# Attention with a gated residual on one Trainium2 core: output-weight sums spread over twelve blocks, and a reordered end stage

## The chip, the cores and the metric

The kernel runs on one core of one Trainium2 chip. The metric is the device time of one execution in microseconds, the median of several runs. A profile is one execution, recorded by the hardware profiler. TensorE is called PE in the profile (its weight loads PEld), VectorE is DVE, ScalarE is ACT, GpSimd is POOL and SyncE is SP; a "q" behind the name is the engine's own queue, on which DMA issues stand.

## What is computed

One sequence x of 2048 tokens with 1024 channels, all in float32. After a layer norm without gain, two branches work on the normalised xn:

```
xn  = layernorm(x)
qkv = xn @ wqkv                       # 32 heads of 32 channels
s   = softmax(q k^T / sqrt(32)) v @ wo
r   = xn @ w_r                        # one score per token
idx = the 8 tokens with the largest r
y   = (silu(xn[idx] @ w_gate) * (xn[idx] @ w_up)) @ w_down * sigmoid(r[idx])
g   = silu(xn + scatter(y at idx))
out = x + s * g
```

## The kernel before, in words

**Precision.** A float32 operand is held as two float16 parts, high and low, and a product is taken as three float16 products (high-high, high-low, low-high), each as four matmuls of 32 weight columns (`narrow`, L282). A guard at the very end checks in four conditions that the ranges allow this (denominators, their inverses, largest weights, low parts); if it fails, `_general` computes everything again.

**Attention.** The 32 heads make 8 groups g of four heads. A block (g, qb) is one group with 512 queries (qb from 0 to 3), 32 blocks in all; a block has 16 units kt, one for each 128 keys. A unit takes the scores (L282, tile `sc`), their exponential on ScalarE (L413, tile `pt`), an addition into the block's running sum of exponentials on VectorE (L420; the sum lives in the `pt` tile of unit 0, five such tiles rotate) and the product with v (L427, tile `oa`). Between these matmuls stand pieces of the next projections (`fill`).

**Denominators.** One unit after a block's end, `fold` stores the running sum into the DRAM buffer a_d (L461, on SyncE's queue) and adds its halves three times with accumulating DMAs on GpSimd's queue (L463). `fold_load` and `fold_rows` bring the 16 rows back and add them; `reciprocals` inverts on VectorE (L479), stores to r_d (L483) and loads it spread over the partitions as `rb` (L488); `normalise` multiplies (L497), `split_o` makes the two parts (L503, L505). `sums` is the other way to the denominators: four matmuls with ones into one bank (L445), a copy on ScalarE (L447), a small store and load (L452, L453). Before the change only block (7, 0) uses it. After the very last block's `rb` the whole of r_d is loaded as `rec` (L491) for the guard.

**Output projection in the end.** For query blocks 2 and 3 (the last eight tiles of 128 tokens) the projection with wo is taken as seven half-size products of sums and differences ("forms") of attention blocks (tiles `sf`, from s_d) and of wo blocks (tiles `tf`, from t_d), which VectorE puts together (L956 to L1004). The forms of wo come from t_f: for each i of 0 to 3, four planes of 512 columns of sums of wo blocks i and 4+i, made in DRAM. Before the change plane 0 holds form 3, plane 1 form 2, plane 2 form 4 and plane 3 form 1 (`T_AT`). In block (1, i) `wo_first` loads all four planes (1 MB, unit 9, SyncE, L745), and `wo_more` accumulates three planes, three planes and one plane (768, 768 and 256 KB; units 11, 13 and 15; GpSimd, L750).

**The end stage.** After the last attention unit come 79 steps on TensorE (`products`): steps 0 to 15 are form 7 (four tiles of 128 tokens, four pieces each, 12 matmuls a piece; ScalarE copies them out, L992), 16 to 27 product 4, 28 to 39 product 6, 40 to 51 product 5, 52 to 63 product 2, 64 to 72 product 3 for three tiles, 73 to 78 product 3 for the last tile in two halves of 256 columns. A tile of a product is three steps of 16 matmuls into one bank of PSUM, and three single banks rotate. After each step the functions placed there with `then(n, ...)` are issued; a function that returns (k, f) has f issued k steps later.

**Gates.** For a tile of 128 tokens `gate_load` loads x as z (L794) and, on GpSimd, clears the tile `up` (L796) and gathers the routed rows into it (L797); three `up` buffers rotate. `gate_sum` normalises z on ScalarE (L806); then one function a step: z + up on VectorE (L809), tanh on ScalarE (L813), the end of silu on VectorE (L814). Before the change the four gates of query block 3 are loaded at steps 22, 24, 26 and 28 and summed at 32, 34, 36 and 38. `written` adds the gated result to x (tile `xo`, loaded by `x_load`, L1018) on VectorE (L936) and stores it (L937).

**Order.** PE, VectorE, ScalarE, SyncE and GpSimd issue in the program order of the code up to `order.close()`. The guard stands behind that line (L1391 to L1409), and its instructions are placed by the framework: in the profile its reductions over `rec` (L1394 to L1396) stand on VectorE's queue inside product 6.

Of the kernel before, what the change touches and what calls it, by code (L numbers as in the profile page):

```python
# [9 lines left out]
F32 = mybir.dt.float32  # L10
# [4 lines left out]
ALU = mybir.AluOpType  # L15
AX = mybir.AxisListType
RED = bass_isa.ReduceOp

P = 128
S = 2048  # L20
D = 1024
# [6 lines left out]
NB = S // 512  # L28
KT = D // P
NG = H // 4  # L30
# [13 lines left out]
KSB = 8  # L44
PTB = 5
HLB = 3
# [59 lines left out]
def _fast(ctx, tc, x, wqkv, wo, w_r, w_gate, w_up, w_down, out, dram, y_d, slot_d, ok_i,  # L106
# [322 lines left out]
        if kt:  # L429
            PT.pop(u)  # L430

    DN = {}

    def unload(g, qb):

# [39 lines left out]
        return reciprocals(g, qb)  # L475

    def reciprocals(g, qb):
        dr = DN[g, qb]
        nc.vector.reciprocal(dr[:, 1], dr[:, 0])  # L479
        rows = r_d[g * NB + qb]  # L480

        def store():
            nc.sync.dma_start(rows.rearrange("j (b q) -> (j b) q", q=16), dr[:, 1])  # L483
            return 4 if (g, qb) == (L, NB - 1) else 1, spread

        def spread():
            rb = DN[g, qb] = sb.tile([P, 512], F32, name="rb", tag="rb", bufs=1)
            nc.sync.dma_start(rb, bass.AP(tensor=rows.tensor, offset=rows.offset, ap=[[512, 4], [0, 32], [1, 512]]))  # L488
            if g == NG - 1 and qb == NB - 1:
                RT["rec"] = sb.tile([P, 512], F32, name="rec", tag="hl", bufs=HLB)  # L490
                nc.sync.dma_start(RT["rec"], r_d.rearrange("b j q -> (b j) q"))  # L491

        return 1, store

    def normalise(g, qb):
        o32 = OA[g, qb]
# [54 lines left out]
    RT = {}  # L551

    def route_load(t):
        if t == 0:
# [183 lines left out]

    WO = {}

    def wo_times(k, h, n):
        return bass.AP(tensor=wo.tensor, offset=wo.offset + k * P * D + 512 * h, ap=[[D, P], [0, n], [1, 512]])
# [118 lines left out]


    SF, TF, PR, XO = {}, {}, {}, {}
    T_AT = {1: 3, 2: 1, 3: 0, 4: 2}

    def form_tiles(f, form, two, name, part=None):
        if two:
# [53 lines left out]
    def tail_items():  # L921
        items = []
        v = nc.vector
        low, high = slice(0, 512), slice(512, D)

        def row(name, tt):
            if tt == 0:
# [3 lines left out]
        def gated(y, z, scale):  # L931
            v.scalar_tensor_tensor(z, y, scale, z, op0=ALU.mult, op1=ALU.mult)

        def written(t, tt, qb):
            o = XO[qb, tt]
            v.tensor_add(o, o, GT[qb][:, tt])  # L936
            nc.sync.dma_start(out[t * P:(t + 1) * P, :], o)  # L937

        def whole(n, tt, j):


            z_a, z_b = (GT[q][:, tt] if q in GT else None for q in (2, 3))
            if j == 0:
                PR["b"] = psm.tile([P, 512], F32, name="wop", tag="m")
            bank = PR["b"]
            terms(n, tt, bank, 4 * j, 4 * j + 4)
            if j < 2:
                return
            if n == 1:
                if tt % 2 == 0:  # L950
                    PR["p1", tt // 2] = sb.tile([P, 2, 512], F32, name="p1", tag=f"w16_{tt // 2}")
                nc.scalar.activation(PR["p1", tt // 2][:, tt % 2], bank, AF.Copy)
            elif n == 4:
                if tt % 2 == 0:
                    PR["g", tt // 2] = sb.tile([P, 2, 512], F32, name="g", tag="qs", bufs=2)
                v.tensor_add(PR["g", tt // 2][:, tt % 2], PR["h"][:, tt], bank)  # L956
            elif n == 6:
                u, h, y = row("u", tt), PR["h"][:, tt], PR["g", tt // 2][:, tt % 2]
                v.tensor_tensor(u, bank, PR["p1", tt // 2][:, tt % 2], op=ALU.subtract)
                v.tensor_add(y, u, y)  # L960
                gated(y, z_a[:, low], WOD)
                v.tensor_add(h, u, h)
            elif n == 5:
                u, h = PR["u"][:, tt], PR["h"][:, tt]
                v.tensor_add(h, h, bank)
                v.tensor_add(u, u, bank)  # L966
                gated(h, z_a[:, high], -WOD)
                written(8 + tt, tt, 2)
            elif n == 2:
                y = PR["p1", tt // 2][:, tt % 2]  # L970
                v.tensor_add(y, y, bank)
                gated(y, z_b[:, low], WOD)
                if tt == 3:
                    o = XO[3, 3]
                    v.tensor_add(o[:, low], o[:, low], z_b[:, low])
                    nc.sync.dma_start(out[S - P:S, low], o[:, low])
                    u = PR["u"][:, tt]
                    gated(z_b[:, high], u, WOD)
                    v.tensor_add(o[:, high], o[:, high], u)
            elif n == 3:  # L980
                y = PR["u"][:, tt]
                v.tensor_add(y, y, bank)
                gated(y, z_b[:, high], WOD)
                written(12 + tt, tt, 3)

        def lines(i, tt):

# [24 lines left out]
        items += [lambda a=(h, j): last(*a) for h in range(2) for j in range(3)]  # L1012
        return first, items

    def x_load(qb, tt, tag):
        t = 4 * qb + tt
        XO[qb, tt] = sb.tile([P, D], F32, name="xo", tag=tag, bufs=2)
        nc.sync.dma_start(XO[qb, tt], x[t * P:(t + 1) * P, :])  # L1018


# [5 lines left out]
    def on(g, qb, kt, fn, *a):  # L1026
        side.setdefault((g, qb, kt), []).append(lambda: fn(*a))
# [111 lines left out]
    then(6, form_whole, "s", 2, False)  # L1139
    then(8, form_whole, "t", 2, False)  # L1140
    then(18, form_whole, "s", 1, True)
    then(20, form_whole, "t", 1, True)
    then(30, fold_load, L, 3)
    then(35, fold_rows, L, 3)
    then(38, form_load, L, 3)
    then(46, normalise, L, 3)
    then(47, split_o, L, 3)
    then(48, form_sum, L, 3)
    then(49, form_split, L, 3, 0, 3)
    then(44, form_tiles, SF, 4, False, "sf")  # L1150
    for i in range(4):
        then((45, 46, 47, 55)[i], form_fetch, "s", 4, i)
    for tt in range(4):
        then((30, 31, 40, 49)[tt], x_load, 2, tt, "qs" if tt == 2 else "wr")
        then((54, 55, 58, 61)[tt], x_load, 3, tt, ("wr", "qs", "qs", "wr")[tt])

# [224 lines left out]
    for n, f in enumerate(products):  # L1381
        clock[0], ready = len(units) + n, due.pop(len(units) + n, [])
        go(f)
        for h in ready + tail.pop(n, []):
            go(h)
    assert not due and not tail and not any(k[0] > L for k in side)

    order.close()


    fl = const.tile([P, 10], F32, name="fl")  # L1391
    nc.gpsimd.partition_all_reduce(am, am, channels=P, reduce_op=RED.max)
    rec = RT["rec"]
    nc.vector.tensor_reduce(fl[:, 0:1], rec, axis=AX.X, op=ALU.add)  # L1394
    nc.vector.reciprocal(rec, rec)
    nc.vector.tensor_reduce(fl[:, 1:2], rec, axis=AX.X, op=ALU.add)  # L1396
    nc.vector.tensor_reduce(fl[:, 2:3], am, axis=AX.X, op=ALU.min)
    nc.vector.tensor_scalar(fl[:, 0:1], fl[:, 0:1], REC_MAX, None, op0=ALU.is_lt)
    nc.vector.tensor_scalar(fl[:, 1:2], fl[:, 1:2], DEN_MAX, None, op0=ALU.is_lt)
    nc.vector.tensor_scalar(fl[:, 2:3], fl[:, 2:3], W_MIN, None, op0=ALU.is_ge)  # L1400
# [160 lines left out]
```

## Time and profile before

| | us |
|---|---|
| median of 3 runs | 1674.81 (1670.83 to 1676.37) |
| the profiled execution, its own time | 1679.71 |
| its span, from the first to the last instruction | 1677.9 |
| PE busy / DVE busy / ACT busy / POOL busy | 1607.2 / 1444.3 / 1195.0 / 162.7 |
| mean granted TensorE clock | 0.987 of full speed |

The profile's rows read as follows. A row of the timeline has its start, its length, the engine, the line of the code, the operation, the tiles (out<-in) and the shape; in brackets behind it stands how long the engine was idle just before and what ended that (`<-`). Times are microseconds from the start of the span. Rows of one line and shape are put together in the groups: count, total, mean in ns, idle time before. A row of the waits says who waited for what, for how long in total, how many times, and the longest. The chain is the sequence of work that ended last, each piece with its start and length. A busy PE is not PE at its peak, since the ends of matmuls are modelled.

### The profile page before, as it was taken

What the parts mean: (1) busy time and instruction counts of PE and PEld (TensorE: products, weight loads), DVE (VectorE), ACT (ScalarE), POOL (GpSimd) and SP (SyncE); (2) the same over time, 40 slices, a digit from 0 to 9 for tenths busy, and PEclk for the clock granted to TensorE, in tenths of its full rate; (3) what the DMA queues carried; (4) which work ended last, traced back from release to release, by engine and by line L of the source; (5) the groups of instructions that cost most, each with busy time, mean ns of one, the idle gap of its engine ahead of it and who ended that gap; (6) DMA issues with size and microseconds to landing.
All of it is one profiled execution on the core that took longest, in us unless ns stands there. A gap on an engine that the chain in (4) does not pass through costs nothing.

```text
span 1677.9 us, 59438 instructions
## 1 busy us (share of the span) xinstructions
PE 1607.2 (96%) x26945; PEld 830.0 (49%) x26945; DVE 1444.3 (86%) x1219; ACT 1195.0 (71%) x1339; POOL 162.7 (10%) x160
## 2 busy tenths in 40 slices
PE   9999999998899999999999999999999999999955
PEld 7644444454444455555555555555444444555522
DVE  8488999898889999999999988788899999787675
ACT  6677777777677777888888877777777778665420
POOL 3400000111000000000000000000001001212020
PEclk9999999999999999999999999999999999999979
DMA  9934565888954465667666687778888897647735
GB/s 291 201 94 134 146 165 151 206 200 192 207 133 103 118 167 150 168 171 191 165 178 172 180 249 213 206 217 203 225 238 231 235 236 241 177 138 211 270 117 184
DMA packets 272598, 313.52 MB, mean 187 GB/s; under 512 B 111702, under 2 KB 202118, under 8 KB 268370
## 3 DMA queue, kind: packets, MB, share of 16 engines
q1 hardware_dynamic: 257778, 273.68, 55.0%
q0 software_dynamic: 14560, 35.96, 13.7%
q8 instruction: 213, 3.49, 0.9%
q14 instruction: 47, 0.39, 0.1%
HBM read 224.28 MB, written 127.32 MB: 210 GB/s over the span
## 4 chain that ended last, share of the span: by engine, by line
PE 73%; DMA 14%; DVE 7%; issue 2%; SPq 2%; ACT 1%; POOL 1%; DVEq 0%; POOLq 0%; ACTq 0%
PE sc L282 22%; PE oa L427 21%; PE proj L282 15%; PE vp L282 6%; PE wop L282 5%; DMA a_d<-pt 3%; DMA a_d<-a_d 3%; DVE pt L420 3%; PE ffn L684 1%; DMA t_f<-in_A_wo_dram 1%; DMA wf<-in_B_w_up_dram 1%; ACT pt L413 1%; PE vp L329 1%; PE py L715 1%; DMA xt<-xh 1%
## 5 line engine op out<-in xcount | busy, mean ns | idle before, releaser
L413 ACT ACTIVATE pt<-sc 128x1024 f32<-128x1024 f32 x1024 | 998.1, 1026 | 335.5 <-PE sc L282 231.6
L420 DVE TENSOR_TENSOR pt<-pt 128x2048 f32<-128x2048 f32 x480 | 1095.2, 2284 | 49.9 <-ACT pt L413 29.3
L282 PE MATMUL sc<-qs,ks 128*32 128x512 f16 x8192 | 622.7, 380 | 21.8 <-ACT pt L413 19.9
L427 PE MATMUL oa<-pt,v 128*32 128x512 f32 x4096 | 533.1, 593 | 0.0
L282 PE MATMUL proj<-xt,w 128*32 128x512 f16 x5664 | 420.8, 380 | 0.0
L282 PEld LDWEIGHTS <-ks 128*32 128x32 f16 x8192 | 234.4, 97 | 187.1 <-issue 41.3
L282 PEld LDWEIGHTS <-w 128*32 128x32 f16 x5664 | 161.8, 97 | 234.3 <-issue 138.7
L463 POOL DMA_DIRECT2D a_d<-a_d x93 | 75.7, 814 | 1204.2 <-DMA a_d<-pt 833.6
L282 PEld LDWEIGHTS <-xt 128*32 128x32 f16 x4608 | 127.7, 97 | 105.8 <-issue 78.4
L427 PEld LDWEIGHTS oa<-pt,v 128*32 128x32 f32 x4096 | 131.1, 110 | 97.5 <-issue 0.9
L282 PE MATMUL vp<-w,xt 128*32 128x256 f16 x4608 | 173.1, 273 | 0.0
L282 PE MATMUL wop<-wo,ot 128*32 128x512 f16 x1920 | 111.0, 379 | 3.4 <-DVE u L966 2.6
L282 PEld LDWEIGHTS <-ot 128*32 128x32 f16 x2112 | 62.9, 97 | 70.2 <-issue 23.0
L380 DVE SCALAR_TENSOR_TENSOR hl<-proj,hl 128x512 f16<-128x512 f32 x61 | 42.0, 688 | 42.8 <-ACT hl L379 42.6
L282 PEld LDWEIGHTS <-sf 128*32 128x32 f16 x816 | 24.8, 103 | 49.0 <-issue 19.8
L497 DVE TENSOR_TENSOR o<-o,rb 128x512 f32<-128x512 f32 x32 | 22.0, 688 | 29.6 <-DMA rb<-r_d 29.6
L329 PE MATMUL vp<-w,xt 128*128 128x256 f16 x384 | 43.9, 273 | 2.5 <-DMA xt<-xh 2.4
L282 PE MATMUL wop<-tf,sf 128*32 128x512 f16 x384 | 25.5, 429 | 18.8 <-DVE u L966 11.1
L329 PEld LDWEIGHTS <-xt 128*128 128x128 f16 x384 | 37.1, 98 | 8.6 <-DMA xt<-xh 3.1
L379 ACT ACTIVATE hl<-proj 128x512 f16<-128x512 f32 x61 | 36.4, 596 | 5.0 <-PE proj L282 4.2
L684 PE MATMUL ffn<-wf,xst 128*32 128x224 f32 x512 | 35.9, 353 | 2.2 <-DMA wf<-in_B_w_gate_dram 1.6
L684 PEld LDWEIGHTS ffn<-wf,xst 128*32 128x32 f32 x512 | 16.2, 110 | 41.6 <-issue 35.5
(177 smaller groups left out, 757.1 us busy)
## 6 DMA issues: line engine op xcount, KB each, us to landing
a_d<-pt SPq DMA_DIRECT2D x31, 1024.0 KB
st<-hl SPq DMA_DIRECT2D x64, 256.0 KB
ks<-st SPq DMA_DIRECT2D x128, 128.0 KB
qs<-st SPq DMA_DIRECT2D x128, 128.0 KB
a_d<-a_d POOLq DMA_DIRECT2D x31, 512.0 KB, 6.7
wf<-in_B_w_gate_dram SPq DMA_DIRECT2D x32, 448.0 KB
wf<-in_B_w_up_dram SPq DMA_DIRECT2D x32, 448.0 KB
wd<-in_B_w_down_dram SPq DMA_DIRECT2D x32, 448.0 KB
```

What stands on the lines that cost most here:

```text
L282: nc.tensor.matmul(out[c], w[:, c], x, **flags)
L329: nc.tensor.matmul(box["ps"][:, tt], xt[:, xi, k, t % 4 * P:(t % 4 + 1) * P], w[:, :, wi, k, :], start=(n == 0), stop=(n == 23))
L379: nc.scalar.activation(hl[:, 0], ps, AF.Copy, scale=KQ)
L380: nc.vector.scalar_tensor_tensor(hl[:, 1], ps, KQ, hl[:, 0], op0=ALU.mult, op1=ALU.subtract)
L413: nc.scalar.activation(PT[u][:, 2 * hf:2 * hf + 2], ps, AF.Exp, bias=0.0, scale=ESC)
L420: nc.vector.tensor_add(ACC[g, qb], ACC[g, qb], PT[u])
L427: nc.tensor.matmul(OA[g, qb][32 * j:32 * j + 32, :], VT[g, kt // 2][:, kt % 2, 32 * j:32 * j + 32], PT[u][:, j, :], start=(kt == 0), stop= ...
L463: nc.gpsimd.dma_start(a_d[0:n], a_d[n:2 * n], accum_op=ALU.add, max_dma_last_dim=4096)
L497: nc.vector.tensor_mul(o32, o32, DN.pop((g, qb)))
L684: nc.tensor.matmul(box[i][32 * j:32 * j + 32, :], RT["xst"][:, k, :], wt[:, j * FQ:(j + 1) * FQ], start=(k == 0), stop=(k == KT - 1))
L715: nc.tensor.matmul(box["py"][32 * q:32 * q + 32, :], box["ht"][:FH, i, 32 * j:32 * j + 32], wt[:FH, q * 256:(q + 1) * 256], start=(n == 0) ...
```

## The change

- **Sums of output weights.** The planes of t_f are now form 1, 3, 2 and 4 in this order. For each i: two planes are loaded (512 KB, SyncE) at unit 5 of block 3i, counted over all blocks; two planes are accumulated (512 KB, GpSimd) at its unit 10; plane 1 is copied to planes 2 and 3 (two copies of 256 KB, DRAM to DRAM, SyncE) at its unit 15; two planes are accumulated at unit 10 of block 3i+1; one plane at unit 10 of block 3i+2. So the transfers lie in blocks 0 to 11 instead of 4 to 7.
- **Denominators of the last block** by `sums` at step 3 and `reciprocals` at step 16 in place of `fold` at 2, `fold_load` at 30 and `fold_rows` at 35; `normalise` to `form_split` move from steps 46 to 49 to steps 30 to 34.
- **Gates of query block 3**: loaded at units 14 and 15 of the last block and at steps 1 and 6, summed at steps 7, 10, 14 and 18.
- **Guard**: the 124 rows of the first 31 blocks are loaded as `rec` at step 5 and reduced, inverted and reduced again at steps 12, 13 and 20; the last block's values come from the small tile `dr` at step 19.
- **Residual additions** (`written`) on GpSimd, and their stores five steps later; the stores of the last tile stay at once, but its first half's is also five steps later.
- **Sums of products 5, 2 and 3** are written back into the product's own bank of PSUM (in product 5 for h alone; the number of additions stays).
- **x loads** of query block 2 at steps 26, 27, 32, 33, of block 3 at 34, 35, 46, 47, in other buffers; the sf tiles of form 4 are fetched at steps 42 to 45 (before 45, 46, 47 and 55).

The diff, cut to its core:

```diff
+    def check_load():
+        RT["rec"] = sb.tile([P, 512], F32, name="rec", tag="hl", bufs=HLB)
+        nc.sync.dma_start(RT["rec"][0:REC], r_d[0:NG * NB - 1].rearrange("b j q -> (b j) q"))
+        RT["fl"] = const.tile([P, 12], F32, name="fl")
+        nc.vector.memset(RT["fl"], 0.0)
+    def check_sum(n):
+        nc.vector.tensor_reduce(RT["fl"][0:REC, n:n + 1], RT["rec"][0:REC], axis=AX.X, op=ALU.add)
+    def check_turn():
+        nc.vector.reciprocal(RT["rec"][0:REC], RT["rec"][0:REC])
+    def check_last():
+        for n in range(2):
+            nc.vector.tensor_reduce(RT["fl"][:, 8 + n:9 + n], RT["dr"][:, 1 - n], axis=AX.X, op=ALU.add)
...
-    def wo_first(i):
-        nc.sync.dma_start(t_f[i], wo_times(i, 1, 4))
-    def wo_more(i, n):
-        to, src = ((slice(0, 3), wo_times(4 + i, 1, 3)), (slice(1, 4), wo_times(i, 0, 3)),
-                   (slice(2, 3), wo_times(4 + i, 0, 1)))[n]
-        nc.gpsimd.dma_start(t_f[i][:, to], src, accum_op=ALU.add, max_dma_last_dim=4096)
+    def wo_sums(i, n):
+        if n == 0:
+            nc.sync.dma_start(t_f[i][:, 0:2], wo_times(i, 1, 2))
+        elif n == 1:
+            nc.gpsimd.dma_start(t_f[i][:, 0:2], wo_times(i, 0, 2, 4 * P * D + 512), accum_op=ALU.add,
+                                max_dma_last_dim=4096)
+        elif n == 2:
+            for m in (2, 3):
+                nc.sync.dma_start(t_f[i][:, m], t_f[i][:, 1])
+        elif n == 3:
+            nc.gpsimd.dma_start(t_f[i][:, 2:4], wo_times(i, 0, 2), accum_op=ALU.add, max_dma_last_dim=4096)
+        else:
+            nc.gpsimd.dma_start(t_f[i][:, 3], wo_times(4 + i, 0, 1)[:, 0], accum_op=ALU.add, max_dma_last_dim=4096)
...
-            v.tensor_add(o, o, GT[qb][:, tt])
-            nc.sync.dma_start(out[t * P:(t + 1) * P, :], o)
+            nc.gpsimd.tensor_tensor(o, o, GT[qb][:, tt], op=ALU.add)
+            return 5, lambda: nc.sync.dma_start(out[t * P:(t + 1) * P, :], o)
...
-                v.tensor_add(h, h, bank)
                 v.tensor_add(u, u, bank)
-                gated(h, z_a[:, high], -WOD)
-                written(8 + tt, tt, 2)
+                v.tensor_add(bank, h, bank)
+                gated(bank, z_a[:, high], -WOD)
+                return written(8 + tt, tt, 2)
...
-        on(1, i, 9, wo_first, i)
-        for n in range(3):
-            on(1, i, (11, 13, 15)[n], wo_more, i, n)
+        for n, (b_, k) in enumerate(((0, 5), (0, 10), (0, 15), (1, 10), (2, 10))):
+            on(*divmod(3 * i + b_, NB), k, wo_sums, i, n)
...
-                then(22 + 2 * tt, gate_load, qb, tt)
-                then(32 + 2 * tt, gate_sum, qb, tt)
+                if tt < 2:
+                    at(nxt - 2 + tt, gate_load, qb, tt)
+                else:
+                    then((1, 6)[tt - 2], gate_load, qb, tt)
+                then((7, 10, 14, 18)[tt], gate_sum, qb, tt)
...
-    then(2, fold, L, 3)
+    then(3, sums, L, 3)
+    then(5, check_load)
+    then(12, check_sum, 0)
+    then(13, check_turn)
+    then(16, reciprocals, L, 3)
+    then(19, check_last)
+    then(20, check_sum, 1)
```

More of the change, by code (lines that the diff above doesn't have):

```diff
@@ L430, in values @@
             PT.pop(u)
-    DN = {}
+    DN, RT = {}, {}
+    REC = 4 * (NG * NB - 1)
     def unload(g, qb):
@@ L477, in reciprocals @@
     def reciprocals(g, qb):
-        dr = DN[g, qb]
+        dr = RT["dr"] = DN[g, qb]
         nc.vector.reciprocal(dr[:, 1], dr[:, 0])
@@ L488, in spread @@
             nc.sync.dma_start(rb, bass.AP(tensor=rows.tensor, offset=rows.offset, ap=[[512, 4], [0, 32], [1, 512]]))
-            if g == NG - 1 and qb == NB - 1:
-                RT["rec"] = sb.tile([P, 512], F32, name="rec", tag="hl", bufs=HLB)
-                nc.sync.dma_start(RT["rec"], r_d.rearrange("b j q -> (b j) q"))
         return 1, store
+    def check_load():
[10 more added lines that the diff above has]
+            nc.vector.tensor_reduce(RT["fl"][:, 8 + n:9 + n], RT["dr"][:, 1 - n], axis=AX.X, op=ALU.add)
     def normalise(g, qb):
@@ L863, in _fast @@
     SF, TF, PR, XO = {}, {}, {}, {}
-    T_AT = {1: 3, 2: 1, 3: 0, 4: 2}
+    T_AT = {1: 0, 2: 2, 3: 1, 4: 3}
     def form_tiles(f, form, two, name, part=None):
@@ L923, in tail_items @@
         v = nc.vector
-        low, high = slice(0, 512), slice(512, D)
+        low, high, later = slice(0, 512), slice(512, D), []
         def row(name, tt):
@@ L964, in whole @@
                 u, h = PR["u"][:, tt], PR["h"][:, tt]
-                v.tensor_add(h, h, bank)
                 v.tensor_add(u, u, bank)
-                gated(h, z_a[:, high], -WOD)
-                written(8 + tt, tt, 2)
+                v.tensor_add(bank, h, bank)
+                gated(bank, z_a[:, high], -WOD)
+                return written(8 + tt, tt, 2)
             elif n == 2:
-                y = PR["p1", tt // 2][:, tt % 2]
-                v.tensor_add(y, y, bank)
-                gated(y, z_b[:, low], WOD)
+                v.tensor_add(bank, PR["p1", tt // 2][:, tt % 2], bank)
+                gated(bank, z_b[:, low], WOD)
                 if tt == 3:
@@ L975, in whole @@
                     v.tensor_add(o[:, low], o[:, low], z_b[:, low])
-                    nc.sync.dma_start(out[S - P:S, low], o[:, low])
+                    later.append(lambda: nc.sync.dma_start(out[S - P:S, low], o[:, low]))
                     u = PR["u"][:, tt]
@@ L979, in whole @@
                     v.tensor_add(o[:, high], o[:, high], u)
+                    return 5, later.pop()
             elif n == 3:
[L981 to L984, printed above, removed]
+                v.tensor_add(bank, PR["u"][:, tt], bank)
+                gated(bank, z_b[:, high], WOD)
+                return written(12 + tt, tt, 3)
         def lines(i, tt):
@@ L1013, in tail_items, with x_load @@
         return first, items
-    def x_load(qb, tt, tag):
+    def x_load(qb, tt, tag, bufs):
         t = 4 * qb + tt
-        XO[qb, tt] = sb.tile([P, D], F32, name="xo", tag=tag, bufs=2)
+        XO[qb, tt] = sb.tile([P, D], F32, name="xo", tag=tag, bufs=bufs)
         nc.sync.dma_start(XO[qb, tt], x[t * P:(t + 1) * P, :])
@@ L1137, in _fast @@
     then(0, form_whole, "t", 4, False)
-    then(2, fold, L, 3)
-    then(6, form_whole, "s", 2, False)
+    then(3, sums, L, 3)
+    then(4, form_whole, "s", 2, False)
+    then(5, check_load)
     then(8, form_whole, "t", 2, False)
[L1141 to L1150, printed above, removed]
+    then(12, check_sum, 0)
[3 more added lines that the diff above has]
+    then(20, check_sum, 1)
+    then(18, form_load, L, 3)
+    then(22, form_whole, "s", 1, True)
+    then(24, form_whole, "t", 1, True)
+    then(30, normalise, L, 3)
+    then(31, split_o, L, 3)
+    then(33, form_sum, L, 3)
+    then(34, form_split, L, 3, 0, 3)
+    then(41, form_tiles, SF, 4, False, "sf")
     for i in range(4):
-        then((45, 46, 47, 55)[i], form_fetch, "s", 4, i)
+        then(42 + i, form_fetch, "s", 4, i)
     for tt in range(4):
-        then((30, 31, 40, 49)[tt], x_load, 2, tt, "qs" if tt == 2 else "wr")
-        then((54, 55, 58, 61)[tt], x_load, 3, tt, ("wr", "qs", "qs", "wr")[tt])
+        then((26, 27, 32, 33)[tt], x_load, 2, tt, "ks", KSB)
+        then((34, 35, 46, 47)[tt], x_load, 3, tt, ("wr", "wr", "qs", "qs")[tt], 2)
     for b in range(NG * NB):
@@ L1385, in _fast @@
             go(h)
+    for n in sorted(due):
+        for h in due.pop(n):
+            h()
     assert not due and not tail and not any(k[0] > L for k in side)
     order.close()
-    fl = const.tile([P, 10], F32, name="fl")
+    fl = RT["fl"]
     nc.gpsimd.partition_all_reduce(am, am, channels=P, reduce_op=RED.max)
[L1393 to L1396, printed above, removed]
     nc.vector.tensor_reduce(fl[:, 2:3], am, axis=AX.X, op=ALU.min)
+    nc.vector.tensor_add(fl[:, 0:2], fl[:, 0:2], fl[:, 8:10])
     nc.vector.tensor_scalar(fl[:, 0:1], fl[:, 0:1], REC_MAX, None, op0=ALU.is_lt)
```

5 lines of the change are left out of this document (2 added, 3 removed).

## The prediction

> **What bounds the kernel now.** I read the page first, then the windows by stage, TensorE's waits, the chain, and last the timeline of the end.
>
> ```profile
> span 1677.9 us, 59438 instructions
> PE 1607.2 (96%) x26945; PEld 830.0 (49%) x26945; DVE 1444.3 (86%) x1219; ACT 1195.0 (71%) x1339; POOL 162.7 (10%) x160
> 147.00:190.00 43.00, 43.00 (x772) 20.70 (x768) 39.54 (x26) 33.41 (x38) 1.61 (x2) 1.00 0.51 141
> 280.00:323.00 43.00, 39.96 (x724) 19.56 (x720) 36.25 (x25) 30.73 (x35) 4.93 (x5) 1.00 0.87 201
> 1567.00:1581.00 14.00, 12.55 (x232) 6.70 (x228) 8.84 (x8) 6.37 (x9) 0.00 (x0) 1.00 1.01 356
> 1567.00:1678.00 111.00, 71.97 (x1240) 36.61 (x1232) 68.34 (x95) 17.09 (x20) 12.09 (x12) 0.87 0.60 201
> ```
>
> The last four rows are windows: the stretch and its length, the busy time (and instructions) of TensorE, of its weight loads, of VectorE, ScalarE and GpSimd, then the granted clock, the DMA share and GB/s. TensorE bounds the whole, but not everywhere. An ordinary block has it busy for 43.00 of 43.00 us with the DMA engines at 0.51. Two stretches fall short: the blocks that carry the sums of the output weights (share 0.87, TensorE 39.96 of 43), and the end, where it works 71.97 of 111.00 us, at a mean clock of 0.87. TensorE's waits from 95 to 480 us are one row (in total, times, longest):
>
> ```profile
> PE sc L282 <- ACT pt L413: 16.3, 3, 8.8
> ```
>
> The chain says where one of the three waits came from:
>
> ```profile
> 345.88 9.67 DMA t_f<-in_A_wo_dram
> 361.70 9.44 DMA a_d<-a_d
> 383.15 8.79 DMA dr<-a_d
> 392.88 6.98 DMA r_d<-dr
> 401.12 8.15 DMA a_d<-pt
> ```
>
> Accumulations into t_f run up to the next fold; the fold that follows on GpSimd is slow, dr and r_d are late on SyncE's queue, and so the next block's fold store (a_d<-pt) starts at 401 us and holds a buffer of pt that ScalarE needs. In the end stage the chain runs over VectorE:
>
> ```profile
> 1568.85 8.60 PE L282 MATMUL y<-tf,sf 128*32 128x512 f16 x156
> 1568.83 2.29 DVE L420 TENSOR_TENSOR pt<-pt 128x2048 f32<-128x2048 f32 x1
> 1581.03 10.55 PE L282 MATMUL wop<-tf,ot 128*32 128x512 f16 x192
> 1598.24 0.77 POOL L463 DMA_DIRECT2D a_d<-a_d  x1 [6.87 <-DMA a_d<-a_d]
> 1609.05 1.23 DVE L809 TENSOR_TENSOR z<-z,up 128x1024 f32<-128x1024 f32 x1 [2.94 <-DMA up<-y_d,slot_i]
> 1611.66 4.38 PE L282 MATMUL wop<-tf,sf 128*32 128x512 f16 x48 [7.13 <-DVE u L959]
> 1613.15 0.48 SPq L491 DMA_DIRECT2D rec<-r_d  x1
> 1618.93 0.69 DVE L1394 TENSOR_REDUCE fl<-rec 128x1 f32<-128x512 f32 x1 [2.40 <-DMA rec<-r_d]
> 1620.13 3.35 DVE L1395 RECIPROCAL rec<-rec 128x512 f32<-128x512 f32 x1
> 1630.49 5.20 PE L282 MATMUL wop<-tf,sf 128*32 128x512 f16 x48 [11.13 <-DVE u L966]
> 1666.18 1.49 PE L282 MATMUL wop<-wo,sf 128*32 128x256 f16 x48 [1.09 <-DVE u L982]
> 1671.52 1.13 SPq L1005 DMA_DIRECT2D out_dram<-xo  x2
> ```
>
> The last gates' gathers stand on GpSimd's queue behind the fold's third accumulation (1598.24), VectorE stands in front of them, TensorE waits 7.13 us; then VectorE waits for rec, inverts it, and TensorE waits 11.13 us. The rows show what a wait costs besides: 48 matmuls took 4.38 and 5.20 us right behind the two waits, where 192 without one took 10.55, 2.6 for 48.
>
> **The change, part by part: the sums of the output weights.** Four blocks with a 1 MB load and three accumulations become twelve with one transfer (two copies of one plane in four of them). What is queued behind: on SyncE the copies at unit 15 wait for GpSimd's accumulation of unit 10, and behind them stand the next block's loads and its fold store. A unit is 2.70 us (the two rows below lie 43.15 us apart, 16 units), so the wait has 13.5 us of cover against a landing of 7.6 to 11.1:
>
> ```profile
> 659.14 0.87 PE vp L282 x32
> 702.29 0.87 PE vp L282 x32
> DMA to landing us min/median/max: 7.6/9.8/11.1
> ```
>
> GpSimd's queue is free for every fold, since no accumulation is issued after unit 10. The extra DMA share of 0.87 - 0.51 = 0.36 in four blocks is spread over twelve, some 0.12 each. If that leaves no fold late, 16.3 us go; if the same waits come back elsewhere, nothing. I take 3 us left, near the quiet rows (0.51 with no loss): -13 us.
>
> **The end: the last denominators** come by four matmuls and two small transfers instead of the fold. The trace has that path once:
>
> ```profile
> 1393.01 0.56 SPq L452 DMA_DIRECT2D d_d<-ds  x1
> 1396.04 0.38 SPq L453 DMA_DIRECT2D dr<-d_d  x1
> 1401.72 0.25 DVE L479 RECIPROCAL dr<-dr 128x16 f32<-128x16 f32 x1 [0.28 <-DMA dr<-d_d]
> ```
>
> 8.7 us from store to reciprocal: from 1574 (the matmuls at step 3, about 1572, then ScalarE's copy) until 1583. The four matmuls take TensorE less than a tile's 2.6 us. GpSimd's queue is then free: the first gathers stand before the end's first matmul (1568.85), not behind the fold's accumulation at 1598.24.
>
> **Gates and guard first.** Nothing of the four gates' work goes away; it moves under form 7 and product 4, where VectorE was nearly idle. The guard's load of rec is now queued on SyncE behind dr, which waits for d_d: by the row 1393.01 to 1396.04, three microseconds after a store that ScalarE's copy lets go at about 1574, and behind four sf loads, so I put its issue at 1580. The load took 5.75 us (1613.15 to 1618.90); in the fuller queues of 1580 I take 6: rec lands at R = 1586 (1582 to 1592). VectorE, in program order, is done with what stands before check_sum by 1581 (L420 until 1571.1, seven gate steps of 1.22, some waiting), so it waits about 5 us, and behind it stand the last gates and all of product 4's additions. Durations:
>
> ```profile
> L814 DVE SCALAR_TENSOR_TENSOR z<-up,z 128x1024 f32<-128x1024 f32 x16 | 19.4, 1220 | 3.4 <-ACT up L813 3.4
> L936 DVE TENSOR_TENSOR xo<-xo,z 128x1024 f32<-128x1024 f32 x7 | 8.6, 1225 | 0.2
> L960 DVE TENSOR_TENSOR g<-u,g 128x512 f32<-128x512 f32 x4 | 2.8, 689 | 0.1
> L505 DVE SCALAR_TENSOR_TENSOR ot<-o,ot 128x512 f16<-128x512 f32 x4 | 2.7, 684 | 0.7 <-ACT ot L503 0.7
> L1004 DVE TENSOR_TENSOR xo<-xo,z 128x256 f32<-128x256 f32 x2 | 0.9, 426 | 0.1
> L271 POOL TENSOR_SCALAR wraw<-wraw 128x1024 f32<-128x1024 f32 x1 | 2.8, 2822 | 18.6 <-ACT w L261 18.6
> L229 POOL TENSOR_TENSOR xh<-xin,xh 128x1024 f16<-128x1024 f32 x12 | 25.7, 2141 | 18.2 <-ACT xh L223 12.2 <-DVE rn L192 6.0
> ```
>
> From R: sum 0.7, gate end 1.2, reciprocal 3.35, gate sum 1.2, small reciprocal 0.25, a wait of 0.8 for ScalarE's tanh (L814's 3.4 are such waits), gate end 1.2, first addition of product 4 0.7: 9.4, so 1595.4. There are three single banks: TensorE, three tiles into product 4 at 1581.0 + 3 x 2.6 = 1588.8, waits 6.6 us for it. VectorE needs 5.6 more (a gate 2.4, two sums 1.1, three additions 2.1) to 1601.0, then product 6: 16 operations of 0.69 and, for the last block's attention, four of 0.69 with two waits of 0.7 for ScalarE: 15.2, to 1616.2. Up to there VectorE is the bound.
>
> **Additions on GpSimd, sums in the bank.** Product 5 falls from 0.69 x 3 + 1.23 = 3.3 to 2.1 us of VectorE per tile, under TensorE's 2.6, and product 3 from 2.6 to 1.4. The first tile of product 5 is off VectorE at 1618.3, which frees the bank for its fourth; from there TensorE is the bound: 2.6 + 4 x 2.6 + 3 x 2.6 + 2 x 1.5 = 23.8, to 1642.1. It ended at 1667.7 (1666.18 + 1.49), so -25.6. Writing a result into a bank has no row; I take the 0.69 of L960, and up to 0.85 three of them stay under 2.6. GpSimd has no addition with float32 out: 2.14 at L229, up to the 2.82 of L271, against one tile each 2.6 us, so it keeps up or lags by less than 1 us.
>
> **Stores five steps later** cost nothing while loads go first; the x loads of the last block are issued 12 to 20 steps earlier. Behind TensorE's end stand two operations of 0.43 (L1004), half a store pair's 1.13 and the landing: the last issue ended at 1672.65 and the span at 1677.9, 5.25 later. That is 6.5 us instead of 10.2: -3.7. The lower clock behind the 6.6 us wait costs 0 to 1.6; I take +1. Sum of the end: -28.
>
> The profiled execution took 1679.7: 1679.7 - 13 - 28 = 1638.7. It lies 4.9 above the median of 1674.8 (1670.8 to 1676.4), so against the median the same sum gives 1633.8, and I forecast 1634. The case's own range is 1624 (TensorE never waits: 1568.85 + 10.6 + 4 x 10.55 + 3 x 2.6 + 3.0 = 1632.4 for its end instead of 1642.1) to 1643 (R = 1592 and lagging GpSimd).
>
> Two rules of the Trainium skill speak against parts of this. "DMA: Bandwidth & Descriptors", under why a DMA increments its semaphore by 16, says that a transfer is split over the largest number of engines up to 16 that divides its rows. The new rec has 124 rows, so 4 engines; as an estimate from that page's bandwidth per engine, 62 KB on each takes 1.6 us more, and the sum by it would be 1636. No run here shows it yet. The other rule is the third rival's.
>
> **The rivals.**
> 1. The early waits only spread (0.17). For: two copies now stand right ahead of every third fold. Against: cover 13.5 against 11.1. The 13 us stay: 1647.
> 2. The gates and the guard are issued first but their data still come late, so VectorE stands in front of product 4 as it stood in front of product 6 (0.09). For: the four up tiles share three buffers, and the DMA engines are full at the start of the end stage (1.01 from 1567 to 1581). R = 1598: 12 us more, 1646.
> 3. GpSimd's additions hold VectorE (0.12). The trace shows such a hold:
>
> ```profile
> 55.24 0.17 DVE L187 TENSOR_SCALAR by<-rn 128x2 f32<-128x2 f32 x1
> 58.19 2.13 POOL L229 TENSOR_TENSOR xh<-xin,xh 128x1024 f16<-128x1024 f32 x1 [0.79 <-ACT xh L223]
> 58.28 2.06 DVE L187 TENSOR_SCALAR by<-rn 128x2 f32<-128x2 f32 x1
> ```
>
> The same operation took 0.17 or 2.06 us, until GpSimd ended. Of VectorE's operations beside the seven additions, three in the fourth tile of product 2 and the last two have no bank among their operands; three holds of 2.1: 1640. The page "SBUF — State Buffer", under who interferes with whom, says that a VectorE instruction with two SBUF inputs and a GpSimd one that reads SBUF shut each other out for the whole instruction; the row at 58.28 agrees for another kind.
> 4. Slower (0.05): the copies at unit 15 do wait, and hold SyncE and with it the fold store in block after block. The four old blocks lost 16.3 / 4 = 4.1 each, the worst wait was 8.8. With 8.8 in four and 4.1 in eight: 68 instead of 16.3, +52 - 28 = +24, 1699. It decides from (28 + 16.3) / 12 = 3.7 us a block.
>
> **How the numbers follow.** Forecast 0.55, rivals 0.17, 0.09, 0.12, 0.05, and 0.02 for no difference. 0.3% (5 us) is about what a measurement can tell. Only rival 4 is slower: faster 0.93, same 0.02, slower 0.05. The range goes from 1621 (TensorE never waits, no early loss left) to 1650, past rivals 1 to 3.
>
> **What would show it.** Right: no wait of sc for pt above 2 us before 600; VectorE idle some 5 us before check_sum; one TensorE wait of 4 to 8 us in product 4, none at product 5; the 0.69 us gated rows on a bank; GpSimd additions near 2.1 us; span end 6 to 7 us after the last matmul. Wrong: SyncE waiting at the copies for in_A_wo transfers; rec landing past 1592; a wait on product 3 for sf; VectorE rows of 2 us beside GpSimd's.

## The result, and the profile after

The changed kernel takes 1635.3 us in the median (1634.4 to 1636.8, 4 runs) against 1675.6 us (1670.8 to 1677.2, 4 runs) for the kernel before; the ratio is 0.9765 with a 95% interval of 0.9744 to 0.9787. The profiled execution took 1636.8 us, its span 1635.1. That is 42.8 us less span than before, and the two places where it was saved are those of the prediction. In microseconds from the start of each span:

| | before | after | difference |
|---|---|---|---|
| end stage begins (first matmul of form 7) | 1568.85 | 1551.05 | -17.8 |
| from there to TensorE's end | 98.8 | 72.7 | -26.1 |
| from TensorE's end to the end of the span | 10.2 | 11.3 | +1.1 |
| the end stage, both together | 109.05 | 84.05 | -25.0 |

The head of the page of the changed kernel:

```profile
span 1635.1 us, 59480 instructions
PE 1598.8 (98%) x26953; PEld 823.1 (50%) x26953; DVE 1438.5 (88%) x1215; ACT 1193.8 (73%) x1340; POOL 177.1 (11%) x164
```

Three of its windows (the stretch and its length, busy time of PE, PEld, DVE, ACT, POOL, then granted clock, DMA share, GB/s):

```profile
147.00:190.00 43.00, 43.00 (x772) 20.70 (x764) 39.57 (x26) 33.44 (x37) 2.84 (x3) 1.00 0.61 155
280.00:323.00 43.00, 43.00 (x772) 20.76 (x768) 39.58 (x26) 33.36 (x38) 3.78 (x5) 1.00 0.66 154
1551.00:1635.10 84.10, 65.71 (x1215) 35.00 (x1204) 57.74 (x89) 16.27 (x19) 24.12 (x14) 0.94 0.63 218
```

The block from 280 to 323 us, which lost 3 us before at a DMA share of 0.87, now has TensorE busy throughout at 0.66; the block from 147 pays for it with 0.61 instead of 0.51 and loses nothing. TensorE's waits say the same: the first row below is all of 480 to 600 us (from 85 to 480 there is none), the other three are the end stage:

```profile
PE sc L282 <- ACT pt L413: 0.6, 1, 0.6
...
PE wop L282 <- DVE g L974: 2.9, 1, 2.9
PE y L282 <- ACT h L1009: 2.6, 2, 1.5
PE wop L282 <- DVE z L950: 1.5, 1, 1.5
```

What was a wait of 7 and one of 11 us is now one of 2.9. All of TensorE's waits in the end stage add up to 28.7 us before (the largest row, `u` L966, has 13.7) and to 7.0 now. The timeline of the end stage, in the order in which the prediction worked it out (start, length, engine and line, operation; in brackets the idle time before and what ended it):

```profile
1551.05 2.78 PE L282 MATMUL y<-tf,sf 128*32 128x512 f16 x48
1560.52 0.33 SPq L495 DMA_DIRECT2D rec<-r_d  x1
1567.00 0.69 DVE L500 TENSOR_REDUCE fl<-rec 124x1 f32<-124x512 f32 x1 [4.47 <-DMA rec<-r_d]
1575.42 0.68 DVE L974 TENSOR_TENSOR g<-h,wop 128x512 f32<-128x512 f32 x1
1576.15 4.46 PE L282 MATMUL wop<-tf,ot 128*32 128x512 f16 x48 [2.92 <-DVE g L974]
1600.27 2.77 PE L282 MATMUL wop<-tf,sf 128*32 128x512 f16 x48 [1.53 <-DVE z L950]
1613.23 10.56 PE L282 MATMUL wop<-wo,sf 128*32 128x512 f16 x240
1618.34 7.02 POOL L954 TENSOR_TENSOR xo<-xo,z 128x1024 f32<-128x1024 f32 x3 [4.30 <-DVE z L950]
1623.01 2.62 DVE L1021 TENSOR_TENSOR xo<-xo,z 128x256 f32<-128x256 f32 x1
1626.01 0.43 DVE L1021 TENSOR_TENSOR xo<-xo,z 128x256 f32<-128x256 f32 x1
1627.40 0.38 SPq L1022 DMA_DIRECT2D out_dram<-xo  x1
```

VectorE stands 4.47 us in front of the guard's first sum until rec has landed; product 4's first addition (L974) ends at 1576.1 and releases TensorE; from 1580 on TensorE runs with one wait of 1.53 us in product 5. The last row but four ends with TensorE at 1623.8. Behind it one of two equal additions (L1021) takes 2.62 us and the other 0.43: the long one starts with GpSimd's last addition, which begins at 1623.02 (1618.34 plus two thirds of 7.02) and ends at 1625.4; the held one ends at 1625.6.

### The profile page after: what moved, and what is told of

Same layout as the page of the kernel before. It is cut to its first block, busy times and chain, and to the rows that moved or that the text cites. A ratio compares the mean times of both kernels' runs of the same rounds, so it can differ in the third digit from the quotient of the medians.

```text
span 1635.1 us, 59480 instructions
## 1 busy us (share of the span) xinstructions
PE 1598.8 (98%) x26953; PEld 823.1 (50%) x26953; DVE 1438.5 (88%) x1215; ACT 1193.8 (73%) x1340; POOL 177.1 (11%) x164
## 4 chain that ended last, share of the span: by engine, by line
PE 75%; DVE 8%; DMA 6%; issue 6%; SPq 2%; POOL 2%; ACT 1%; DVEq 0%; POOLq 0%; ACTq 0%
PE sc L282 22%; PE oa L427 22%; PE proj L282 16%; PE vp L282 7%; DVE pt L420 5%; PE wop L282 4%; DMA a_d<-pt 1%; PE ffn L696 1%; PE vp L329 1%; POOL up L815 1%; DMA a_d<-a_d 1%; DMA xt<-xh 1%; SPq L395 1%; PE py L727 1%; DMA wf<-in_B_w_gate_dram 1%
## 5 line engine op out<-in xcount | busy, mean ns | idle before, releaser
L266 DVE SCALAR_TENSOR_TENSOR w<-wraw,w 128x1024 f16<-128x1024 f32 x23 | 28.0, 1217 | 3.7 <-ACT w L261 3.6
```

The source lines that it names most:

```text
L266: nc.vector.scalar_tensor_tensor(hl[:, 1], WR[c, g], WS, hl[:, 0], op0=ALU.mult, op1=ALU.subtract)
```

## The experiments

Each kernel was compared with the kernel before on one chip. The start of the end stage differs by up to 7.5 us between kernels that have no early waits, and the kernel before itself ran from 1664 to 1678 us, so a few microseconds of the end are read from the traces. Even there, the four kernels with one and the same end stage (changed, end only, old sums spread, new sums packed) take 84.1 to 86.1 us, so a difference of some 2 us between two rows shows nothing by itself. In the table, the first four columns are from the profiled execution (end stage begins; from there to TensorE's end; from that to the end of the span; the end stage together), the last two from all timed runs.

| kernel | begins | to PE's end | rest | end stage | median us | ratio (95%) |
|---|---|---|---|---|---|---|
| before | 1568.85 | 98.8 | 10.2 | 109.0 | 1675.6 | 1 |
| changed | 1551.05 | 72.7 | 11.3 | 84.1 | 1635.3 | 0.9765 (0.9744 to 0.9787) |
| sums only | 1548.53 | 96.9 | 9.7 | 106.6 | 1654.9 | 0.9891 (0.9857 to 0.9925) |
| end only | 1568.71 | 73.1 | 11.9 | 85.0 | 1654.3 | 0.9885 (0.9855 to 0.9915) |
| old sums spread | 1554.09 | 74.0 | 11.9 | 85.9 | 1639.2 | 0.9790 (0.9758 to 0.9822) |
| new sums packed | 1568.68 | 74.8 | 11.3 | 86.1 | 1652.1 | 0.9872 (0.9840 to 0.9903) |
| additions on VectorE | 1550.36 | 74.8 | 9.4 | 84.1 | 1634.2 | 0.9777 (0.9750 to 0.9803) |
| last three on VectorE | 1548.01 | 73.1 | 9.4 | 82.5 | 1632.9 | 0.9778 (0.9750 to 0.9806) |
| guard rows early | 1546.55 | 69.5 | 11.2 | 80.8 | 1634.3 | 0.9783 (0.9755 to 0.9811) |
| both | 1551.68 | 69.5 | 9.5 | 78.9 | 1632.9 | 0.9762 (0.9735 to 0.9788) |
| gates late | 1547.40 | 81.2 | 11.5 | 92.7 | 1643.7 | 0.9845 (0.9821 to 0.9870) |
| fold for the last block | 1550.90 | 81.8 | 11.6 | 93.4 | 1645.7 | 0.9853 (0.9827 to 0.9879) |
| guard at its old place | 1547.58 | 74.7 | 11.6 | 86.2 | 1635.5 | 0.9793 (0.9768 to 0.9817) |
| both, stores at once | 1547.82 | 68.8 | 8.7 | 77.5 | 1630.4 | 0.9764 (0.9744 to 0.9785) |

### Do the two parts add up?

The kernel before with the new sums alone, and the changed kernel with the old sums:

```diff
# sums only: the kernel before with
-        on(1, i, 9, wo_first, i)
-        for n in range(3):
-            on(1, i, (11, 13, 15)[n], wo_more, i, n)
+        for n, (b_, k) in enumerate(((0, 5), (0, 10), (0, 15), (1, 10), (2, 10))):
+            on(*divmod(3 * i + b_, NB), k, wo_sums, i, n)
# end only: the changed kernel with the same lines the other way round
```

> The kernel before with the twelve-block sums of output weights alone; the end stage stays as before. Theory (the early waits come from accumulations that lie beside the folds of blocks 4 to 7): TensorE's waits of sc for pt before 600 us fall from 16.3 us to under 2, the end stage starts some 17 us earlier (about 1551), and the time is 13 to 18 us below the kernel before, about 1660. Rival (most of what the whole change saved lies in the end stage, and the profiled execution of before was an unlucky one in its early blocks): under 8 us.

> The changed kernel with the old sums (1 MB and three accumulations in blocks 4 to 7). Theory: the two parts add up, so the end stage alone gives some 25 us from its first matmul to the end of the span (84 instead of 109 us) and the early waits of 16 us are back: about 1651. Rival: early waits shift what is late in the end, so that the two parts together are more or less than their sum by over 5 us.

Measured: 17.4 us less than before for the sums (1672.3 to 1654.9) and 18.1 for the end (1672.3 to 1654.3); the changed kernel gave 2.35%, 39.3 us of 1672.3, so the parts and the whole agree within 4 us. The end alone came to 1654, not to the 1651 expected. In the traces the sums alone bring the end stage forward by 20.3 us and leave it at 106.6 us, and the end alone leaves its beginning at 1568.71 and takes 85.0. That is 24.1 us less than the trace of the kernel before, where the medians have 18.1; the profiled execution of the kernel before (1679.7 us) lay above its medians, and the same end stage took 106.6 us in `sums only`, so the 25 us of the first table may be a few too many. TensorE's waits for pt before 600 us are 1.1 us with the new sums and 15.1 with the old ones. Both theories hold in the traces; each part does its work in its own place.

### Is it the place or the bytes of the sums?

The new transfers move less (2.3 instead of 2.8 MB for each i) and lie elsewhere. Two kernels separate this:

```diff
# old sums spread: the old transfers, at the new places
+        on(*divmod(3 * i, NB), 5, wo_first, i)
+        for n in range(3):
+            on(*divmod(3 * i + n, NB), 10, wo_more, i, n)
# new sums packed: the new transfers, at the old place
+        for n, k in enumerate((9, 11, 13, 14, 15)):
+            on(1, i, k, wo_sums, i, n)
```

> The changed kernel with the old transfers (1 MB, then 768, 768 and 256 KB), but spread: load at unit 5 and first accumulation at unit 10 of block 3i, the others at unit 10 of the next two blocks. Same bytes as before, other places. Theory (the place decides: no accumulation runs into a fold): within 3 us of the changed kernel, 1635 to 1638, no wait of sc for pt above 2 us before 600. Rival (the bytes decide: 11.3 MB instead of 9.2 into t_f): a good part of the 16 us comes back, 1643 or more.

> The changed kernel with the new, smaller transfers put into the four blocks 4 to 7 (units 9, 11, 13, 14 and 15). Fewer bytes, the old place. Theory (the place decides): waits of sc for pt of 8 to 20 us before 600 are back, 1645 to 1655, and SyncE waits at the copies besides. Rival (the bytes decide): within 4 us of the changed kernel.

The old bytes spread out: the only wait of TensorE for pt between 85 and 600 us,

```profile
PE sc L282 <- ACT pt L413: 0.8, 2, 0.6
```

and the window of one of the blocks that carried the sums in the kernel before (there at a share of 0.85 with TensorE busy throughout; it lost its 3 us in the windows on either side, from 280 and from 366):

```profile
323.00:366.00 43.00, 43.00 (x772) 20.77 (x768) 40.56 (x30) 34.06 (x38) 3.25 (x4) 1.00 0.64 173
```

The new bytes packed into the four blocks, the same wait,

```profile
PE sc L282 <- ACT pt L413: 11.4, 4, 4.7
```

and the same window:

```profile
323.00:366.00 43.00, 39.77 (x696) 20.95 (x692) 37.48 (x27) 30.61 (x35) 5.57 (x6) 0.97 0.81 200
```

The place decides: with the old bytes at the new places the waits are gone, with the new bytes at the old place 11.4 us of them stay (15.1 in `end only`, with the old bytes there) and the end stage begins at 1568.68, where it did before. Whether the bytes cost something besides stays open: `old sums spread` begins its end stage at 1554.09, later than every kernel with the new transfers at the new places (1546.55 to 1551.68), and its 1639.2 us lie between the 1638 of the theory and the 1643 of the rival. The expected wait of SyncE at the packed copies does not appear among its waits, so that half of the expectation was wrong; it was GpSimd that stood in front of its next accumulation until the copies had landed, 65.5 us in four times.

### What in the end stage carries it?

Three kernels take one part of the end back each: the gates' steps, the fold for the last block, and the guard's reductions behind the written order.

```diff
# gates late
-                if tt < 2:
-                    at(nxt - 2 + tt, gate_load, qb, tt)
-                else:
-                    then((1, 6)[tt - 2], gate_load, qb, tt)
-                then((7, 10, 14, 18)[tt], gate_sum, qb, tt)
+                then(22 + 2 * tt, gate_load, qb, tt)
+                then(32 + 2 * tt, gate_sum, qb, tt)
# fold for the last block
-    then(3, sums, L, 3)
-    then(16, reciprocals, L, 3)
+    then(2, fold, L, 3)
+    then(16, fold_load, L, 3)
+    then(18, fold_rows, L, 3)
# guard at its old place: rec whole, loaded behind the last rb; no check_load to check_sum, and behind order.close()
+    nc.vector.tensor_reduce(fl[:, 0:1], rec, axis=AX.X, op=ALU.add)
+    nc.vector.reciprocal(rec, rec)
+    nc.vector.tensor_reduce(fl[:, 1:2], rec, axis=AX.X, op=ALU.add)
```

> The changed kernel with the four gates of the last query block back at their old steps (loads at 22 to 28, sums at 32 to 38). Theory (the order on VectorE decides, and four gates of 2.45 us belong under form 7 and product 4): TensorE does not wait in product 4 any more, but 9.8 us of gates stand in product 6, where VectorE is the bound, so TensorE's end comes about 5 us later than in the changed kernel and the end stage takes some 89 us instead of 84. Rival (only the free GpSimd queue mattered, since the gathers land in time either way): within 2 us of 84.

> The changed kernel with the last block's denominators by the fold again (fold at step 2, its rows loaded at 16 and added at 18), gates and guard as in the changed kernel. Theory (the fold's three accumulations on GpSimd's queue, some 8 us each behind an 8 us store, hold the last gather and the denominators, and VectorE and SyncE stand in order behind them): a wait of TensorE of 12 to 20 us in product 4, the end stage 96 to 105 us. Rival (the denominators are not needed before product 2, so they may be late): within 4 us of 84.

> The changed kernel with the guard's reductions behind the written order again, on all 128 rows of r_d, loaded behind the last block's rb; the steps check_load to check_sum are left out. Theory: VectorE does not wait for rec ahead of product 4, so TensorE's wait of 2.92 us there goes, but 0.69 + 3.35 + 0.69 us fall where the framework puts them; inside product 6, where VectorE is the bound, that makes the end stage 84 to 90 us, behind it less than 84. Rival (moving the guard was what the end needed): over 90 us.

Gates late: the end stage takes 92.7 us, 8.7 more than in the changed kernel. The wait in product 4 is gone, as expected, and two waits in product 5 are there instead, the first for VectorE's work on product 6 (L977), the second for that on product 5 (L950):

```profile
1570.80 13.14 PE L282 MATMUL wop<-tf,sf 128*32 128x512 f16 x240
1588.56 8.11 PE L282 MATMUL wop<-tf,sf 128*32 128x512 f16 x96 [4.62 <-DVE u L977]
1602.41 5.31 PE L282 MATMUL wop<-tf,sf 128*32 128x512 f16 x48 [5.74 <-DVE z L950]
```

The direction and the place, VectorE's work on product 6, are as the theory has them; the 5 us expected were too few, since the matmuls behind each wait ran slow as well (96 in 8.11 us, where 240 before took 13.14, 5.3 for 96; and 48 in 5.31 instead of 2.77).

Fold for the last block: 93.4 us, 9.4 more. Its timeline on GpSimd, VectorE and TensorE:

```profile
1563.79 0.98 POOL L464 DMA_DIRECT2D a_d<-a_d  x1 [4.07 <-DMA a_d<-pt]
1573.76 0.82 POOL L464 DMA_DIRECT2D a_d<-a_d  x1 [8.98 <-DMA a_d<-a_d]
1578.45 0.77 POOL L464 DMA_DIRECT2D a_d<-a_d  x1 [3.87 <-DMA a_d<-a_d]
1580.46 1.09 POOL L815 DMA_INDIRECT up<-y_d,slot_i  x1 [0.28 <-POOL up L814]
1584.51 0.58 DVE L474 TENSOR_REDUCE dr<-dr 128x16 f32<-128x256 f32 x1 [6.43 <-DMA dr<-a_d]
1587.84 19.83 PE L282 MATMUL wop<-tf,sf 128*32 128x512 f16 x336 [6.93 <-DVE g L974]
```

The last gather stands behind the third accumulation, VectorE stands 6.43 us for dr, and TensorE, one tile further than expected, at the start of product 6, 6.93 us for an addition of product 4: the mechanism of the expectation, with a smaller price than its 12 to 20 us. Form 7 has another part, 6.2 us of waits for ScalarE's copies instead of 2.6; but the kernels with the changed end stage have up to 5.2 there as well, so that part need not be the fold's.

Guard at its old place: 86.2 us, 2.2 more, no more than the spread named above. As expected the wait in product 4 is gone; a larger one stands in front of product 6's second tile, where TensorE waits for an addition of product 4. VectorE's row of the timeline,

```profile
1575.47 0.69 DVE L1419 TENSOR_REDUCE fl<-rec 128x1 f32<-128x512 f32 x1 [4.88 <-DMA rec<-r_d]
```

and the row of TensorE's waits:

```profile
PE wop L282 <- DVE g L977: 5.1, 1, 5.1
```

The framework put the sum between product 4's additions, where VectorE waits 4.88 us for rec. So the written steps saved little over that, if anything; what counts is when rec lands, as the next group shows.

### What is left: rec and the last additions

```diff
# additions on VectorE
-            nc.gpsimd.tensor_tensor(o, o, GT[qb][:, tt], op=ALU.add)
+            v.tensor_add(o, o, GT[qb][:, tt])
# last three on VectorE: the same, only if qb == 3
# guard rows early
-    then(5, check_load)
+    then(1, check_load)
# both: the last two edits together; both, stores at once: and for qb == 3
+            if qb == 3:
+                nc.sync.dma_start(out[t * P:(t + 1) * P, :], o)
+                return
```

> The changed kernel with all seven residual additions back on VectorE (stores still five steps later). Theory (VectorE's order in products 4 and 6 sets TensorE's end, and GpSimd's last addition sets the end of the span): 7 x 1.23 us come back to VectorE, of which it hides all but some 2 us beside TensorE in products 5 to 3, while the hold of 2.2 us on the last tile's addition goes: within 3 us of the changed kernel. Rival (the additions are what VectorE was freed of, so they are the gain): 6 to 9 us slower than the changed kernel.

> The changed kernel with only the three additions of product 3 on VectorE, the four of product 5 still on GpSimd. Theory (the hold): the last tile's first addition takes 0.43 us instead of 2.62, the last 512 KB store goes out earlier, the stretch from TensorE's end to the span's end falls from 11.3 to 7 or 9 us: 2 to 4 us faster than the changed kernel. Rival (the landing of the last stores sets the end whatever engine adds): within 1 us of the changed kernel.

> The changed kernel with the guard's load issued at step 1 instead of step 5, ahead of the two small transfers of the denominators and of product 6's loads on SyncE's queue. Theory (VectorE's wait for rec, 4.47 us, is what delays product 4's additions): rec lands before VectorE comes to it, TensorE's wait of 2.92 us in product 4 and the slow 48 matmuls behind it (4.46 us) go: 3 to 6 us faster. Rival (VectorE's own work in front of product 4 is the bound, or the denominators, now behind a 248 KB load, come late in its place): within 1.5 us.

> Both edits together: guard rows loaded at step 1, and the three additions of product 3 on VectorE. Theory: the two gains add, since one lies before TensorE's end and one behind it: 5 to 9 us faster than the changed kernel, 1626 to 1630. Rival: the earlier end of TensorE only meets VectorE's backlog, and no more than 3 us are left of the sum.

> Guard rows loaded at step 1, the three additions of product 3 on VectorE and their stores issued at once instead of five steps later. Theory (the last 512 KB store is what lands last): its issue moves from 1.2 us behind its addition to right behind it, and the stretch from TensorE's end to the span's end falls from 9.5 to some 8.5 us; end stage 77.5 to 78.5 us; by the median some 4 us under the changed kernel, less sure, since the start of the end stage differs by up to 7 us from run to run. Rival (the landing of the very last small store sets the end): 9.5 us stay.

With all seven additions on VectorE the end stage takes the same 84.1 us: TensorE's end comes 2.0 us later and the rest is 1.9 us shorter. So the additions on GpSimd are worth nothing that shows here; the theory holds. With only the last three on VectorE the rest falls from 11.3 to 9.4 us and TensorE loses 0.4. The two equal operations of the last tile in that kernel, against 2.62 and 0.43 in the changed one:

```profile
L1024 DVE TENSOR_TENSOR xo<-xo,z 128x256 f32<-128x256 f32 x2 | 0.8, 425 | 0.1
```

With the guard's rows loaded at step 1, VectorE hardly waits for them, TensorE does not wait in product 4, and its end comes 3.2 us earlier:

```profile
1546.55 2.78 PE L282 MATMUL y<-tf,sf 128*32 128x512 f16 x48
1551.11 0.33 SPq L495 DMA_DIRECT2D rec<-r_d  x1
1559.83 0.69 DVE L500 TENSOR_REDUCE fl<-rec 124x1 f32<-124x512 f32 x1 [0.25 <-DMA rec<-r_d]
1605.50 10.56 PE L282 MATMUL wop<-wo,sf 128*32 128x512 f16 x240
```

Both edits make 78.9 us, 5.1 less than the changed kernel; 1.6 (last three) and 3.3 (guard rows) alone add up to 4.9. With the stores at once it is 77.5, and the rest falls from 9.5 to 8.7, as expected. In the times this is not shown, and the 2 to 4, 3 to 6 and 5 to 9 us under the changed kernel that were expected of the first three did not come: the ratios of all these kernels, 0.9762 to 0.9783, lie within each other's intervals and that of the changed kernel. The last one's median of 1630.4 (1627.2 to 1631.9) lies below the changed kernel's 1635.3 (1634.4 to 1636.8), but the kernel before was lower too in that comparison (1669.3 instead of 1675.6), so whether it is faster stays open.

## Why the prediction was right

**The sum was right, two of its terms were not.** It gave 1638.7 for a profiled execution and the measured one is 1636.8; by the median 1634 against 1635.3. Of the terms, the early part was put at -13 and is -17.8, the end at -28 and is -25.0. The errors cancel, and that the median was met within 1.3 us is luck. The -17.8 is not sharp either: the kernels without early waits begin the end stage 14.8 to 22.3 us earlier than the kernel before.

**The early waits** were to fall from 16.3 to 3 us; between 85 and 480 us none is left. I kept 3 back for nothing, and did not count what the lower clock after the waits had cost (granted 0.96 in the window from 409 to 452 us and 0.89 from 452 to 498 before, 1.00 in both now). The reason is shown: place alone does it, bytes alone do not. "Twelve with one transfer" was a misreading: block 3i has the load, an accumulation and the two copies, the next two blocks one accumulation each. The cover of 13.5 us for the copies was more than enough, the landing of all transfers of t_f, the copies' source among them, being

```profile
DMA to landing us min/median/max: 6.6/8.0/9.3
```

**The chain on VectorE.** Counted from the first matmul of form 7, rec was to land at 17.2 us and landed at 15.9; VectorE was to wait 5 us and waited 4.47; the first addition of product 4 was to end 9.4 us behind rec and ended 9.1 behind it; TensorE's end was to come at 73.2 us and came at 72.7. The wait in product 4 was to be 6.6 us and was 2.92, under the 4 to 8 named as a sign. Part of that is VectorE, 1.5 us earlier than worked out; the other part is a wait that I did not list: TensorE reached it 2.2 us later, because form 7 took 14.2 us instead of 12.2. It has the four denominator matmuls in it, and the row of waits for ScalarE's copies, 2.6 us where the kernel before had 1.5: the copies of form 7 stand behind the gates' tanh on ScalarE's queue, which waits for VectorE. The step "nothing of the gates' work goes away; it moves under form 7" left out that ScalarE's queue is shared there. The 1.53 us at product 5, where the signs had no wait, are in the sum itself: by it TensorE comes to the fourth tile of product 5 at 1616.2 (1595.4 and eight tiles of 2.6), and the bank is free at 1618.3.

That the load of rec delays product 4 is shown by loading it at step 1: TensorE's end comes 68.8 to 69.5 us behind the first matmul in the three kernels that do so, 72.7 to 74.8 in the six with the same gates, denominators and guard that load it at step 5. That the gates' and the denominators' order carries most of the end is shown by taking each back (8.7 and 9.4 us); guard and additions give nothing beyond the spread. Where the rest of the 25 us lay is only read from the trace of the kernel before: late in its end stage TensorE waited 2.85 us for sf and 1.11 and 1.09 for VectorE, which had stood 9.1 us for an x load (a row of the timeline and one of the groups):

```profile
1654.79 7.70 PE L282 MATMUL wop<-wo,sf 128*32 128x512 f16 x108 [2.85 <-DMA sf<-s_d]
L975 DVE TENSOR_TENSOR xo<-xo,z 128x512 f32<-128x512 f32 x1 | 0.7, 693 | 9.1 <-DMA xo<-in_A_x_dram 9.1
```

No kernel with the changed end has these waits, which points to the earlier x loads and sf fetches; the prediction does not list them, and no run takes them back.

**The rest behind TensorE's end** is the term that failed: 6.5 us predicted, 11.3 measured. The step read "two operations of 0.43, half a store pair's 1.13 and the landing", which adds up to 6.7, and took the landing of 5.25 us from the kernel before. In its place stand 4.0 us until the last issue is done (1623.79 to 1627.78), with a hold of 2.2 us in them (2.62 instead of 0.43), and a landing of 7.3 us behind it (to 1635.1). The hold is the third rival, at one of the five places where it could strike, and its price there was named (2.1 us). The rule of the Trainium skill in "SBUF — State Buffer", under who interferes with whom, that a VectorE instruction with two SBUF inputs is shut out for the whole of a GpSimd one that reads SBUF, agrees with the row at 1623.01: it ends 0.2 us behind GpSimd's addition. The hold is not the whole price, though: with the guard at its old place it fell on the second addition and was 1.2 us (1.62 instead of 0.42), and the rest was 11.6 all the same. What goes with the additions is the landing: 7.3 to 7.9 us in all eight kernels that have product 3's additions on GpSimd, 5.8 to 5.9 in the three that have them on VectorE with the stores still five steps later, and 5.4 with the stores at once as well (1619.90 to 1625.3). So the later stores cost some 0.5 us, and why the landing is longer with GpSimd's additions is not shown.

**Other rivals.** Waits that only spread did not happen. The late data of rival 2 did not happen either: rec landed at 15.9 us, where R = 1598 would have been 29.1. Rival 4 did not happen: SyncE never stood at the copies. The Trainium skill's rule in "DMA: Bandwidth & Descriptors", under why a DMA increments its semaphore by 16, gave 4 engines for the 124 rows and, by the prediction's estimate, a price of 1.6 us; the runs neither show nor exclude it. The 124 rows took 6.46 us (1560.52 to 1566.98) in the changed kernel and up to 9.0 (fold for the last block) where VectorE waited for them, the whole 128 took 5.75 in the kernel before and 7.36 with the guard at its old place (issue at 1568.09, landed at 1575.45), each among other transfers.

**Small terms.** Writing a sum back into its bank costs what I took (L984, 0.69 us each). GpSimd's additions cost 2.36 to 2.39 us, inside the 2.14 to 2.82.

## What to carry to other kernels

When background transfers cost time, look first at what they meet: the same bytes left waits of 0.8 us in all once no accumulation was queued in front of a store that frees a buffer. On an engine that issues in order, a load that a side task waits for delays all the main work queued behind it; issue that load before anything that can block its queue. Keep an offloaded operation away from the last instructions of the program: with GpSimd's additions beside VectorE's last ones the stretch behind TensorE's end was 1.9 us longer here (11.3 instead of 9.4).

## What the runs showed that I had not expected

- One VectorE addition of 128 x 256 took 2.62 us beside a GpSimd addition and 0.43 us without; in the other stages of the end, where one operand of VectorE's operations was a bank of PSUM, they kept their 0.69 us beside GpSimd's 2.36.
- A wait of only 2.92 us was followed by 48 matmuls in 4.46 us instead of 2.77; a wait of 1.53 us in the same stage by none that were slow (48 in 2.77). These draw no line: a wait of 2.29 us in `sums only` was followed by 96 in 7.05 us (twice 2.77 would be 5.5), one of 2.28 in the kernel before by 48 in 2.77.
- The landing of the last store varied from 5.2 to 7.9 us from kernel to kernel, and was longest wherever GpSimd made the additions of product 3.
